# A gated mix of attention and SwiGLU on one core: q and k terms stored once and copied in DRAM, x split behind the last unit, one attention step a beat

## The chip, the cores and the metric

The kernel runs on one core of a Trainium2 chip. Its time is the device time of one execution, in microseconds (us). A core has five engines, each with its own instruction queue: TensorE (PE, matrix products; PEld is its weight load), VectorE (DVE), ScalarE (ACT), GpSimd (POOL) and SyncE (SP), which here issues every DMA. SBUF is the on-chip memory of 128 partitions, PSUM the eight banks that PE writes to; DRAM is the memory outside.

## The reference

```python
x = A_x                                              # 1 x 2048 x 576
g = sigmoid((x * gate_w).sum(-1, keepdims=True))
a = attention_with_memory(x, wq, wk, wv, wo, beta)   # 32 heads of 18, four segments of 512 rows
b = (silu(x @ w_gate) * (x @ w_up)) @ w_down         # 4608 hidden columns
return g * a + (1 - g) * b
```

In each segment a head computes a causal softmax attention over the segment's own 512 rows. It also reads a memory that was summed over the earlier segments, `phi(q) M / phi(q) z` with `phi(t) = t + 1` for positive t and `exp(t)` otherwise; `sigmoid(beta)` weighs the two.

## The kernel before

Single-precision products are made of parts: a number is split into a high part (rounded to PE's fast f32 format) and a rest, and three products, high x high, high x low, low x high, replace one. For the scores, q and k are split into three bf16 terms each, and six pairs of terms are stacked along the contraction: 6 x 18 = 108 rows for a head.

**Stage 1, projections** (lines 205 to 467). For each of four segments: nine chains (`qk`, line 248) of 14 matmuls of 512 columns make q and k for 128 columns of the weights; m = 4 holds 64 columns of q and 64 of k. `qk` makes the three bf16 terms `q3` of the chain (ACT, DVE, ACT, POOL; two buffers) and puts the writes of them to `stk` in DRAM on a list `late`. `stk` has six slots a row: for q the terms hi hi hi, mid mid, lo, and for k hi mid lo, hi mid, hi, so that slot by slot the six pairs meet. Each chain gives three writes (line 267), m = 4 six. `flush` (line 244) issues them from SP a chain later. Then eight value steps (`v_step`, line 272: 14 matmuls of 288 columns, half a head group and 128 rows each), between which stand the memory's products (`mem_step`, line 339). During the values the next segment's x is loaded and split, one chunk a step. In the last segment the eight x chunks of the feed-forward's first half are loaded instead (`x_first`, line 401) and split by 14 functions (`todo`).

**Stage 2, feed-forward and attention together** (lines 470 to 993). The rows are worked in two halves (segments 2 and 3, then 0 and 1). Each half has 36 units, one for each 128 hidden columns. A unit multiplies gate and up weights with x by a scheme of seven products (`seven`, line 883: six matmuls of 512 columns; `rest2` adds two) in place of eight; `w_make` (line 488) builds the seven weight operands in the first half and keeps them in DRAM, from which `w_fetch` takes them in the second. Sums of x chunks for the scheme are made by `x_sum` (POOL), their parts by `split` (ACT, DVE). Every third unit also starts 16 groups of the down projection (`down_group`, line 725: nine matmuls of 288 columns, then a DVE addition to `ya`).

The order is written out by hand. After each of a unit's eight products or pairs of them stands a `tick` (line 920), which calls `beat` (line 830). A beat first runs what was deferred to it (`due`: weight splits, loads, the splits of `hh` and `hl`), then up to SHARE[k] down groups, and between these it adds a credit of TICK[half][busy]; busy means that down groups are waiting. When the credit reaches 1, the next attention step is issued (`att_gen`, line 666). There are 339 steps; 320 of them have scores. When they are out, `c_open` (line 748) loads and splits the output weights over the next 13 beats. In beats 5 and 6, behind the Silu, a unit without groups takes no step (QUIET). With a SHARE of 3 the credit is added twice in a beat.

A step works on a fifth of a pair of heads. `t_bank` (line 606) makes up to 512 columns of transposed scores from blocks named in TPLAN, ACT takes their Exp into `pe` (line 616), POOL masks it, and DVE and POOL split it into two f16 parts (lines 689, 691). `s_bank` (line 565) makes scores for the row maxima of a later pair from blocks in SPLAN, which DVE reduces (line 579). Both share three PSUM banks in turn (5, 6, 7), so the scores of one step wait for the Exp of the step before. Every fifth step also issues 40 small matmuls with the values (lines 641, 643).

Between the halves `BREAK` = 10 beats without a unit run the last 16 groups, with a share of 2. During the first half's last unit and these beats `x_second` (line 849) loads, sums and splits x for the second half. Its `x_slot`s are those of the first half's x, which the last unit still reads.

**Stage 3** (lines 998 to 1028) adds the memory's part, projects with `wo` and mixes with the feed-forward.

In the built program SP uses eight DMA semaphores in turn: a DMA is not issued before the one eight places ahead of it has landed.

Of the kernel before, what the change touches and what calls it, by code (L numbers as in the profile page):

```python
# [20 lines left out]
P = 128  # L21
S = 2048
D = 576
# [18 lines left out]
HALF = ((2, 3), (0, 1))  # L42
TICK = ((0.2, 0.83), (0.64, 0.84))
QUIET = (5, 6)
# [11 lines left out]
def gated_mix(ctx, tc, xT, wf, wd, wv, wo, beta, cmask, ident, bmask, out):  # L56
# [146 lines left out]


    xs_of = {}
    with ExitStack() as st:
# [41 lines left out]
        def qk(s, m, u):  # L248
            t0 = s * L
            t = chain_tile()  # L250
            hi, lo = qw[m]
            products(t, w_stat(hi[:, u], lo[:, u]), x_side(*xs_of[s]))
            q3 = sp.tile([P, 3, L], BF, name="q3")
            qr = sp.tile([P, L], F32, name="qr", bufs=1)
            nc.scalar.activation(q3[:, 0], t, AF.Copy)
            nc.vector.tensor_sub(qr, t, q3[:, 0])  # L256
            nc.scalar.activation(q3[:, 1], qr, AF.Copy)  # L257
            nc.gpsimd.tensor_sub(q3[:, 2], qr, q3[:, 1])  # L258
            if m == 4 or (u == 0 and s > 0) or (u == 1 and s < 3):
                ph = sp.tile([P, L], F32, name=f"ph{m}{u}", bufs=2 if u or m == 4 else 1)  # L260
                phi[s, m, u] = ph
                nc.scalar.activation(ph, t, AF.Relu, scale=-1.0)
                nc.scalar.activation(ph, ph, AF.Exp, scale=-1.0)
                nc.vector.scalar_tensor_tensor(ph, t, 0.0, ph, op0=OP.max, op1=OP.add)
            parts = [(u, m * P, 0, P)] if m < 4 else [(0, 512, 0, 64), (1, 512, 64, 64)]
            for kind, r0, p0, n in parts:
                for c, m in ((0, 3), (3, 2), (5, 1)):
                    z = 3 - m
                    src = q3[p0:p0 + n, 0:m] if kind else q3[p0:p0 + n, z:z + 1].to_broadcast([n, m, L])
                    late.append((stk[kind, r0:r0 + n, c:c + m, t0:t0 + L], src))  # L270

# [150 lines left out]
        for s in range(NSEG):  # L422
            upd = upd_gen(s - 1) if s else None
            for n, (m, u) in enumerate(chains):
                if s == 0:
                    for z in loads.get(n, []):
                        z()
                    if n + 3 < 9:
                        q_split(*chains[n + 3])
                    if n in (6, 7):  # L430
                        v_split(n - 6)
                qk(s, m, u)
                flush(6 if m == 4 else 3)
                if upd is not None and n > 0:
                    next(upd, None)
                if s == 1 and n < 3:
                    masks(*((0, 3), (3, NT), (0, 0))[n])
# [8 lines left out]
            for n in range(8):  # L446
                hf, i = divmod(n, 4)
                flush()
                v_step(s, hf, i)
                if s:  # L450
                    mem_step(s, n // 2, n % 2)
                if s < 3:
                    if n == 0:
                        xs_of[s + 1] = x_tiles(s + 1)
                    if n < 5:
                        raws["x", n] = x_load(s + 1, n)
                    if 1 <= n < 6:
                        x_split(xs_of[s + 1], n - 1, raws["x", n - 1])
                else:
                    if n == 0:  # L460
                        wraw = {0: [w_load(0, u) for u in range(2)]}
                    if n == 4:
                        wraw[1] = [w_load(1, u) for u in range(2)]
                    for _ in range(2 if n in (1, 3, 5) else 1):
                        if len(todo) > 4:
                            todo.pop(0)()
        flush()


    with ExitStack() as st:  # L470
# [5 lines left out]
        def row_tile():  # L476
            return rw.tile([P, L], F32, name="row")


        wraw_of, wops, wrem = wraw, {}, {}  # L480

        def op_tile():
            return wop.tile([P, 2, 2, P], F32R, name="wo_")

        def rem_tile():
            return wop.tile([P, 2, P], F32R, name="wr_", bufs=3)

        def w_make(f):
            g, u = wraw_of.pop(f)
            ops, rem = [None] * 7, [None] * 2  # L490
            wops[0, f], wrem[0, f] = ops, rem
            a11, a12, a21, a22 = g[:, 0:2], g[:, 2:4], u[:, 0:2], u[:, 2:4]
            src = [a11, None, None, a12, None, None, a22]

            def total(j, p, q, sub=True):
                src[j] = rp.tile([P, 2, P], F32, name="ws", bufs=3)
                (nc.gpsimd.tensor_sub if sub else nc.gpsimd.tensor_add)(src[j], p(), q())

            def high(j):
                ops[j] = op_tile()  # L500
                nc.scalar.activation(ops[j][:, 0], src[j], AF.Copy)

            def low(j):
                nc.vector.tensor_sub(ops[j][:, 1], src[j], f32(ops[j][:, 0]))

            def rem_high(z, r):
                rem[z] = rem_tile()
                nc.scalar.activation(rem[z][:, 0], r, AF.Copy)

            def rem_low(z, r):  # L510
                nc.vector.tensor_sub(rem[z][:, 1], r, f32(rem[z][:, 0]))

            def keep(j):
                nc.sync.dma_start(wc[f, j], f32(ops[j]).rearrange("p a k n -> p (a k n)"))

            def rem_keep(z):
                nc.sync.dma_start(rc[f, z], f32(rem[z]).rearrange("p a n -> p (a n)"))

            todo = [(LEAD - 1, lambda: total(1, lambda: a21, lambda: a22, False)),
                    (LEAD, lambda: total(2, lambda: src[1], lambda: a11)),  # L520
                    (LEAD + 2, lambda: total(4, lambda: a11, lambda: a21)),
                    (LEAD + 3, lambda: total(5, lambda: a12, lambda: src[2]))]
            for j in range(7):
                todo += [(LEAD + j, lambda j=j: high(j)), (LEAD + j + 1, lambda j=j: low(j)),
                         (LEAD + j + 2, lambda j=j: keep(j))]
            for z, r in ((0, g[:, 4]), (1, u[:, 4])):
                o = LEAD + 4 + 2 * z
                todo += [(o, lambda z=z, r=r: rem_high(z, r)), (o + 1, lambda z=z, r=r: rem_low(z, r)),
                         (o + 2, lambda z=z: rem_keep(z))]
            return sorted(todo, key=lambda t: t[0])  # L530

# [14 lines left out]

        start = w_make(0)
        while start[0][0] < 8:
# [13 lines left out]
        stack_load(0)  # L562
        SPLAN = [[(0, 0, 3)], [(0, 1, 3)], [(0, 0, 2), (384, 0, 0)], [(0, 1, 2), (384, 1, 0)], [(0, 0, 1), (256, 1, 1)]]

# [38 lines left out]

        TPLAN = [[(0, 0)], [(1, 0)], [(0, 1), (0, 3)], [(1, 1), (1, 3)], [(0, 2), (1, 2)]]

# [48 lines left out]
        def o_step(g):  # L654
# [3 lines left out]
            nc.vector.reciprocal(rz, av[:, :, :, DH])  # L658
            nc.vector.tensor_mul(rz, rz, omg[:, 4 * b:4 * b + 4])
            ob = ap.tile([P, 4, 4 * DH], F32, name="ob", bufs=1)  # L660
# [169 lines left out]
        def beat(k=None, half=0):  # L830
# [4 lines left out]
            for n in range(max(share, 1)):  # L835
                if groups and n < share:
                    down_group(*groups.pop(0))
                if n % 2 or (k in QUIET and not busy):
                    continue
# [9 lines left out]
        def x_second(new, xs):  # L849
# [22 lines left out]
            todo = []  # L872
            for z, loads, at in ((0, ((1, 0), (3, 0), (0, 0), (2, 1)), 2), (1, ((0, 7), (1, 8), (3, 9), (2, 9)), 10)):
                todo += [(o, lambda z=z, q=q: load(z, q)) for q, o in loads]
                for o, j, what in ((0, 0, parts), (1, 1, total), (2, 1, parts), (3, 2, total), (3, 3, parts),
                                   (4, 2, parts), (4, 4, total), (5, 4, parts), (5, 6, total), (6, 5, parts),
                                   (6, 6, parts)):
                    todo.append((at + o, lambda z=z, j=j, what=what: what(z, j)))
            for b in range(2):
                todo += [(9, lambda b=b: rest_load(b)), (13 + b, lambda b=b: rest(b))]  # L880
            return sorted(todo, key=lambda t: t[0])
# [17 lines left out]
        for pos, (half, f) in enumerate(seq):  # L899
# [16 lines left out]
            for o, fn in plan:  # L916
                defer(o + 1, fn)
            step = [0]

            def tick():  # L920
# [38 lines left out]
            nc.scalar.activation(xx, a, AF.Copy)  # L959
            tick()  # L960
            seven(y, w[5], XO[5], False, False)
            rest2(y, wr[0], XS[1])
            nc.scalar.activation(sg1, y, AF.Silu)  # L963
            nc.scalar.activation(sg0, sg0, AF.Silu)
            tick()
# [12 lines left out]
            if f == FT - 1:  # L978
                groups += feed(half, f)
                if half == 0:  # L980
                    for _ in range(BREAK):
                        beat()
                    XO, XS = X2, XS2
# [92 lines left out]
```

## Time and profile before

| | |
|---|---|
| median of 3 runs | 1948.53 us (1942.0 to 1951.9) |
| the profiled execution | 1951.22 us; its span is 1949.5 us |
| mean granted TensorE clock | 0.984 |
| projections, 0 to 259 us | PE is busy in 226.4 of 259 us |
| half one with its break | 259 to 1076 us |
| half two | 1076 to 1860 us |
| the end | 1860 to 1950 us |
| DMA | 344.96 MB in 227878 packets, mean 177 GB/s |

The span runs from the first to the last instruction. A line of a group reads: line, engine, operation, what it writes and reads, count, busy time, mean of one, idle time of the engine before it with what ended most of that. A line of waits reads: who waited for whom, us in total, how often, the longest. A line of the order of time reads: start, length, engine, line, operation, out<-in, count, and in brackets the idle time before it with what ended it. "PE busy" is a model of pipelined matmuls; a PE that is busy is not always at its peak.

### The profile page before, as it was taken

To read this page: it belongs to the slowest core of one execution; us is meant where nothing else is said; L and a number is where in the kernel's file an instruction comes from. 1 tells how busy PE (TensorE), PEld (TensorE's weight loads), DVE (VectorE), ACT (ScalarE), POOL (GpSimd) and SP (SyncE) were. 2 spreads that over 40 slices of the span, in tenths; PEclk is the share of its full clock that TensorE was granted. 3 is DMA by queue.
4 is the path that set the end of the run, shared out by engine and by line. 5 is a ranking of instruction groups with operands and counts; after the bars stand their busy time and mean duration, and the time that the engine had idled before them with its cause. 6 is when DMAs were issued, how large, how long until landed. Compare 5 with 4: busy or idle time off the path is not lost.

```text
span 1949.5 us, 35977 instructions
## 1 busy us (share of the span) xinstructions
PE 1845.1 (95%) x12508; PEld 1554.6 (80%) x12508; DVE 1274.4 (65%) x3064; ACT 947.2 (49%) x1786; POOL 856.5 (44%) x1214
## 2 busy tenths in 40 slices
PE   7899889999999999999997999999999999999999
PEld 6788778778877877888786787787787788778899
DVE  5355377787787778788877766666666766443355
ACT  5555463665466466556654544435444544432211
POOL 2323352454545555555555655555555555400021
PEclk9999999999999999999998999999999999999999
DMA  7565666664565456356645645545544643564444
GB/s 246 180 203 182 214 249 205 216 220 134 180 232 178 154 199 222 134 191 236 216 145 189 208 140 148 156 141 146 152 143 145 184 131 107 167 198 154 137 156 140
DMA packets 227878, 344.96 MB, mean 177 GB/s; under 512 B 38576, under 2 KB 123696, under 8 KB 227696
## 3 DMA queue, kind: packets, MB, share of 16 engines
q1 hardware_dynamic: 227696, 342.66, 54.2%
q8 instruction: 99, 1.62, 0.4%
q14 instruction: 83, 0.68, 0.1%
HBM read 194.33 MB, written 148.24 MB: 176 GB/s over the span
## 4 chain that ended last, share of the span: by engine, by line
PE 73%; DVE 7%; ACT 7%; DMA 5%; issue 4%; POOL 2%; SPq 1%; ACTq 0%; DVEq 0%; POOLq 0%
PE bank L887 28%; PE bank L735 23%; PE bank L893 6%; PE bank L127 5%; PE bank L572 3%; PE bank L612 3%; PE bank L641 2%; ACT L616 1%; DMA xo<-in_xT_dram 1%; PE bank L643 1%; ACT pe L616 1%; DVE xo L105 1%; PE bank L304 1%; POOL p L691 1%; DVE qr L256 1%
## 5 line engine op out<-in xcount | busy, mean ns | idle before, releaser
L691 POOL TENSOR_TENSOR p<-pe,p 128x512 f16<-128x512 f32 x320 | 372.4, 1164 | 598.3 <-DVE p L689 542.4
L735 PE MATMUL bank<-dw,hh 128*128 128x288 f32 x2304 | 482.3, 302 | 21.5 <-DVE ya L740 10.4
L735 PEld LDWEIGHTS bank<-dw,hh 128*128 128x128 f32 x2304 | 378.9, 190 | 45.8 <-DVE ya L740 15.8
L616 ACT ACTIVATE pe<-bank 128x512 f32<-128x512 f32 x320 | 190.4, 596 | 338.2 <-PE bank L612 287.9
L735 PE MATMUL bank<-dw,hl 128*128 128x288 f32 x1152 | 342.1, 297 | 1.1 <-DVE hl L105 1.1
L740 DVE TENSOR_TENSOR ya<-bank,ya 128x288 f32<-128x288 f32 x352 | 160.1, 456 | 228.2 <-PE bank L735 225.2
L579 DVE CUSTOM_DVE_ANT_0 scr<-bank,cm 128x512 bf16<-128x512 f32 (+3 forms) x512 | 248.7, 486 | 10.1 <-PE bank L572 3.3
L735 PEld LDWEIGHTS bank<-dw,hl 128*128 128x128 f32 x1152 | 218.7, 190 | 1.7 <-DVE hl L105 1.7
L689 DVE CAST p<-pe 128x512 f16<-128x512 f32 x320 | 166.4, 521 | 2.8 <-POOL pe L624 2.8
L572 PE MATMUL bank<-kst,qst 108*128 108x512 bf16 (+3 forms) x512 | 126.8, 301 | 30.2 <-ACT pe L616 28.5
L612 PE MATMUL bank<-qst,kst 111*128 111x512 bf16 (+3 forms) x512 | 151.3, 306 | 0.0
L624 POOL TENSOR_SCALAR_AFFINE_SELECT pe<-pe 128x256 f32<-128x256 f32 (+1 forms) x320 | 136.6, 427 | 15.2 <-ACT pe L616 13.3
L955 ACT ACTIVATE row<-bank 128x512 f32<-128x512 f32 x72 | 43.0, 597 | 140.3 <-PE bank L893 140.2
L105 DVE TENSOR_TENSOR hl<-row,hh 128x512 fp32r<-128x512 f32 x72 | 52.5, 729 | 82.9 <-ACT hh L104 82.9
L612 PEld LDWEIGHTS <-kst 111*128 111x128 bf16 x512 | 49.4, 98 | 71.0 <-issue 53.3
L968 DVE TENSOR_TENSOR bank<-bank,row 128x512 f32<-128x512 f32 x72 | 50.3, 698 | 80.8 <-ACT row L963 80.2
L127 PE MATMUL bank<-xo,qhi 128*128 128x512 f32 x288 | 93.6, 406 | 7.4 <-ACT xo L104 5.1
L792 POOL TENSOR_TENSOR o<-o,me 128x576 f32<-128x576 f32 x12 | 17.1, 1428 | 189.0 <-DMA me<-med 180.8
L616 ACT ACT_TABLE_LOAD x59 | 75.7, 1283 | 44.7 <-PE bank L612 42.4
L944 ACT ACTIVATE bank<-bank 128x512 f32<-128x512 f32 x72 | 42.0, 583 | 98.4 <-PE bank L887 87.8
L258 POOL TENSOR_TENSOR q<-qr,q 128x512 bf16<-128x512 f32 x36 | 41.9, 1164 | 106.9 <-ACT q L257 106.0
L959 ACT ACTIVATE bank<-bank 128x512 f32<-128x512 f32 x72 | 41.9, 582 | 96.5 <-PE bank L887 96.5
(2083 smaller groups left out, 4354.4 us busy)
## 6 DMA issues: line engine op xcount, KB each, us to landing
raw<-in_wf_dram SPq DMA_DIRECT2D x72, 320.0 KB
dc<-dw SPq DMA_DIRECT2D x36, 576.0 KB
dw<-dc SPq DMA_DIRECT2D x36, 576.0 KB
qst<-stk SPq DMA_DIRECT2D x64, 216.0 KB
kst<-stk SPq DMA_DIRECT2D x64, 216.0 KB
stk<-q SPq DMA_DIRECT2D x32, 384.0 KB
draw<-in_wd_dram SPq DMA_DIRECT2D x36, 288.0 KB
stk<-q SPq DMA_DIRECT2D x32, 256.0 KB
```

The lines of the kernel that those rows point to most:

```text
L127: nc.tensor.matmul(t, st[n], mv[n], start=(n == 0), stop=(n == 13))
L572: nc.tensor.matmul(t[:, c:c + w], qs[:KR, pr, P * i:P * i + P], ks[:KR, pr, 0:w], start=True, stop=True)
L579: nc.vector.tensor_tensor_reduce(scr[:, :w], t[:, c:c + w], cm[:, L - w:L], 1.0, -3.0e38, OP.add, OP.max, m[:, k:k + 1])
L612: nc.tensor.matmul(t[:, c:c + w], ks[:KR + 3, pr, P * j:P * j + P], qs[:KR + 3, pr, P * j:L], start=True, stop=True)
L616: nc.scalar.activation(pe, t, AF.Exp, scale=SCALE)
L624: nc.gpsimd.affine_select(d, d, pattern=pat, compare_op=OP.is_ge, fill=0.0, base=0, channel_multiplier=-1)
L689: nc.vector.tensor_copy(p1, pe)
L691: nc.gpsimd.tensor_sub(p2, pe, p1)
L735: nc.tensor.matmul(t, p, q[:, cs], start=(n == 0), stop=(n == 3 * CH - 1))
L740: nc.vector.tensor_add(ya[:, i, cs], t, ya[:, i, cs])
L887: nc.tensor.matmul(t, w[:, p, z], x[z][:, q], start=first and n == 0, stop=last and n == 5, skip_group_check=True)
L893: nc.tensor.matmul(t, w[:, p], xs, start=False, stop=p == 1, skip_group_check=True)
```

## The change

1. `q3` of a k chain is stored in the opposite order (lo mid hi). Each chain now writes its three terms to slots 0 to 2 in one DMA; m = 4 writes q in one and k in three. New `copies(s)` fills slots 3 and 4, and 5, of q and k by four DMAs from DRAM to DRAM. They are issued behind value steps 4 to 7 for segments 0 to 2, and in units 2 to 5 of the feed-forward for segment 3. The six pairs of terms are the same.
2. In the last segment's values no x split is done behind step 0 and two behind each of steps 1 to 5. `w_make(0)`, the first unit's weights, moves from behind the values into steps 3 to 7 (its functions moved up in the file unchanged).
3. `beat`: without waiting groups, credit is added once a beat. TICK is changed with it.
4. SPLAN and TPLAN: in three banks the 128-column block comes before the 384-column block.
5. `x_second`: loads and splits are later, the splits all behind the first half's last unit; the first beat of the break takes no down group.
6. Silu of `sg0` is issued a product earlier, ahead of that of `sg1`.
7. The small product for `rz` goes from DVE to POOL.

The order of the program's instructions on PE differs only by item 4 and by where steps and groups fall; the number of matmuls is the same. SP issues 56 DMAs fewer (72 writes less, 16 copies more).

```diff
-TICK = ((0.2, 0.83), (0.64, 0.84))
+TICK = ((0.25, 0.83), (0.6, 0.8))
...
-            nc.scalar.activation(q3[:, 0], t, AF.Copy)
-            nc.vector.tensor_sub(qr, t, q3[:, 0])
+            z0, z2 = (2, 0) if u else (0, 2)
+            nc.scalar.activation(q3[:, z0], t, AF.Copy)
+            nc.vector.tensor_sub(qr, t, q3[:, z0])
             nc.scalar.activation(q3[:, 1], qr, AF.Copy)
-            nc.gpsimd.tensor_sub(q3[:, 2], qr, q3[:, 1])
+            nc.gpsimd.tensor_sub(q3[:, z2], qr, q3[:, 1])
...
-            parts = [(u, m * P, 0, P)] if m < 4 else [(0, 512, 0, 64), (1, 512, 64, 64)]
-            for kind, r0, p0, n in parts:
-                for c, m in ((0, 3), (3, 2), (5, 1)):
-                    z = 3 - m
-                    src = q3[p0:p0 + n, 0:m] if kind else q3[p0:p0 + n, z:z + 1].to_broadcast([n, m, L])
-                    late.append((stk[kind, r0:r0 + n, c:c + m, t0:t0 + L], src))
+            if m < 4:
+                late.append((stk[u, m * P:m * P + P, 0:3, t0:t0 + L], q3))
+            else:
+                late.append((stk[0, 512:D, 0:3, t0:t0 + L], q3[0:64]))
+                for z in range(3):
+                    late.append((stk[1, 512:D, 2 - z, t0:t0 + L], q3[64:128, z]))
+
+        def copies(s):
+            t0 = s * L
+            r = []
+            for kind in range(2):
+                for c, m in ((3, 2), (5, 1)):
+                    z = 3 - m if kind else 0
+                    r.append((stk[kind, :, c:c + m, t0:t0 + L], stk[kind, :, z:z + m, t0:t0 + L]))
+            return r
...
-                flush(6 if m == 4 else 3)
+                flush(4 if m == 4 else 1)
...
-                    for _ in range(2 if n in (1, 3, 5) else 1):
+                    for _ in range(2 if n else 0):
                         if len(todo) > 4:
                             todo.pop(0)()
+                    if n == 3:
+                        start = w_make(0)
+                    for _ in range((0, 0, 0, 0, 3, 3, 6, 6)[n]):
+                        if start[0][0] < 8:
+                            start.pop(0)[1]()
+                if n > 3 and s < 3:
+                    nc.sync.dma_start(*copies(s)[n - 4])
...
-        SPLAN = [[(0, 0, 3)], [(0, 1, 3)], [(0, 0, 2), (384, 0, 0)], [(0, 1, 2), (384, 1, 0)], [(0, 0, 1), (256, 1, 1)]]
+        SPLAN = [[(0, 0, 3)], [(0, 1, 3)], [(384, 0, 0), (0, 0, 2)], [(384, 1, 0), (0, 1, 2)], [(0, 0, 1), (256, 1, 1)]]
...
-        TPLAN = [[(0, 0)], [(1, 0)], [(0, 1), (0, 3)], [(1, 1), (1, 3)], [(0, 2), (1, 2)]]
+        TPLAN = [[(0, 0)], [(1, 0)], [(0, 1), (0, 3)], [(1, 3), (1, 1)], [(0, 2), (1, 2)]]
...
-            nc.vector.tensor_mul(rz, rz, omg[:, 4 * b:4 * b + 4])
+            nc.gpsimd.tensor_mul(rz, rz, omg[:, 4 * b:4 * b + 4])
...
-                if n % 2 or (k in QUIET and not busy):
+                if n % 2 or (not busy and (n or k in QUIET)):
                     continue
...
-            for z, loads, at in ((0, ((1, 0), (3, 0), (0, 0), (2, 1)), 2), (1, ((0, 7), (1, 8), (3, 9), (2, 9)), 10)):
+            for z, loads, at in ((0, ((0, 3), (1, 3), (3, 4), (2, 5)), 8), (1, ((0, 11), (1, 12), (3, 12), (2, 13)), 13)):
                 todo += [(o, lambda z=z, q=q: load(z, q)) for q, o in loads]
-                for o, j, what in ((0, 0, parts), (1, 1, total), (2, 1, parts), (3, 2, total), (3, 3, parts),
-                                   (4, 2, parts), (4, 4, total), (5, 4, parts), (5, 6, total), (6, 5, parts),
-                                   (6, 6, parts)):
+                for o, j, what in ((0, 0, parts), (0, 1, total), (1, 1, parts), (1, 2, total), (1, 3, parts),
+                                   (2, 2, parts), (2, 4, total), (2, 6, total), (3, 4, parts), (3, 5, parts),
+                                   (4, 6, parts)):
                     todo.append((at + o, lambda z=z, j=j, what=what: what(z, j)))
             for b in range(2):
-                todo += [(9, lambda b=b: rest_load(b)), (13 + b, lambda b=b: rest(b))]
+                todo += [(9, lambda b=b: rest_load(b)), (16 + b, lambda b=b: rest(b))]
...
+            if half == 0 and 2 <= f < 6:
+                defer(4, lambda f=f: nc.sync.dma_start(*copies(NSEG - 1)[f - 2]))
...
+            nc.scalar.activation(sg0, sg0, AF.Silu)
             seven(y, w[5], XO[5], False, False)
             rest2(y, wr[0], XS[1])
             nc.scalar.activation(sg1, y, AF.Silu)
-            nc.scalar.activation(sg0, sg0, AF.Silu)
...
-                    for _ in range(BREAK):
-                        beat()
+                    for n in range(BREAK):
+                        beat(None if n else 0)
```

More of the change, by code (lines that the diff above doesn't have):

```diff
@@ L202, in d_load, with op_tile, rem_tile, w_make @@
         return r
+    wraw_of, wops, wrem = {}, {}, {}
+    def op_tile():
+        return wop.tile([P, 2, 2, P], F32R, name="wo_")
+    def rem_tile():
+        return wop.tile([P, 2, P], F32R, name="wr_", bufs=3)
+    def w_make(f):
+        g, u = wraw_of.pop(f)
+        ops, rem = [None] * 7, [None] * 2
+        wops[0, f], wrem[0, f] = ops, rem
+        a11, a12, a21, a22 = g[:, 0:2], g[:, 2:4], u[:, 0:2], u[:, 2:4]
+        src = [a11, None, None, a12, None, None, a22]
+        def total(j, p, q, sub=True):
+            src[j] = rp.tile([P, 2, P], F32, name="ws", bufs=3)
+            (nc.gpsimd.tensor_sub if sub else nc.gpsimd.tensor_add)(src[j], p(), q())
+        def high(j):
+            ops[j] = op_tile()
+            nc.scalar.activation(ops[j][:, 0], src[j], AF.Copy)
+        def low(j):
+            nc.vector.tensor_sub(ops[j][:, 1], src[j], f32(ops[j][:, 0]))
+        def rem_high(z, r):
+            rem[z] = rem_tile()
+            nc.scalar.activation(rem[z][:, 0], r, AF.Copy)
+        def rem_low(z, r):
+            nc.vector.tensor_sub(rem[z][:, 1], r, f32(rem[z][:, 0]))
+        def keep(j):
+            nc.sync.dma_start(wc[f, j], f32(ops[j]).rearrange("p a k n -> p (a k n)"))
+        def rem_keep(z):
+            nc.sync.dma_start(rc[f, z], f32(rem[z]).rearrange("p a n -> p (a n)"))
+        todo = [(LEAD - 1, lambda: total(1, lambda: a21, lambda: a22, False)),
+                (LEAD, lambda: total(2, lambda: src[1], lambda: a11)),
+                (LEAD + 2, lambda: total(4, lambda: a11, lambda: a21)),
+                (LEAD + 3, lambda: total(5, lambda: a12, lambda: src[2]))]
+        for j in range(7):
+            todo += [(LEAD + j, lambda j=j: high(j)), (LEAD + j + 1, lambda j=j: low(j)),
+                     (LEAD + j + 2, lambda j=j: keep(j))]
+        for z, r in ((0, g[:, 4]), (1, u[:, 4])):
+            o = LEAD + 4 + 2 * z
+            todo += [(o, lambda z=z, r=r: rem_high(z, r)), (o + 1, lambda z=z, r=r: rem_low(z, r)),
+                     (o + 2, lambda z=z: rem_keep(z))]
+        return sorted(todo, key=lambda t: t[0])
     xs_of = {}
@@ L460, in gated_mix @@
                     if n == 0:
-                        wraw = {0: [w_load(0, u) for u in range(2)]}
+                        wraw_of[0] = [w_load(0, u) for u in range(2)]
                     if n == 4:
-                        wraw[1] = [w_load(1, u) for u in range(2)]
-                    for _ in range(2 if n in (1, 3, 5) else 1):
+                        wraw_of[1] = [w_load(1, u) for u in range(2)]
+                    for _ in range(2 if n else 0):
                         if len(todo) > 4:
                             todo.pop(0)()
+                    if n == 3:
[5 more added lines that the diff above has]
+                    nc.sync.dma_start(*copies(s)[n - 4])
         flush()
@@ L477, in row_tile @@
             return rw.tile([P, L], F32, name="row")
[L480 to L530, printed above, removed]
         def w_fetch(f):
@@ L545, in w_fetch @@
             return [(j + 2 + late * (j == 6), lambda j=j: one(j)) for j in range(7)] + [(8, lambda: two(0)), (9, lambda: two(1))]
-        start = w_make(0)
         while start[0][0] < 8:
```

## The prediction

> **What bounds the kernel now.** I read the busy times first, then the stages by windows, then the waits of PE stage by stage, then the order of time where PE waits. The first line says that PE is busy for 95% of the span; no other engine passes 65%. So an edit pays only where it removes PE time or a wait of PE, and 1949.5 - 1845.1 = 104.4 us of waits exist at all, in the records.
>
> ```profile
> PE 1845.1 (95%) x12508; PEld 1554.6 (80%) x12508; DVE 1274.4 (65%) x3064; ACT 947.2 (49%) x1786; POOL 856.5 (44%) x1214
> ```
>
> The windows cut this by stage (us, then busy time of PE, PEld, DVE, ACT, POOL, the granted clock, DMA share, GB/s):
>
> ```profile
> 0.00:64.00 64.00, 49.84 (x241) 42.37 (x242) 30.97 (x48) 38.03 (x70) 16.57 (x25) 0.95 0.72 233
> 225.00:259.00 34.00, 23.81 (x161) 23.05 (x159) 22.60 (x54) 17.40 (x41) 19.87 (x19) 0.90 0.60 201
> 259.00:275.00 16.00, 14.21 (x52) 11.03 (x53) 10.44 (x25) 10.34 (x22) 10.15 (x15) 0.79 0.78 276
> 302.00:1022.00 720.00, 692.59 (x4707) 577.25 (x4707) 552.20 (x1333) 405.26 (x805) 360.90 (x518) 0.99 0.56 189
> 1022.00:1076.00 54.00, 41.69 (x300) 35.66 (x299) 39.23 (x86) 23.12 (x41) 31.93 (x37) 0.84 0.56 189
> 1076.00:1692.00 616.00, 594.17 (x4496) 481.98 (x4495) 410.56 (x1063) 292.08 (x479) 337.37 (x508) 1.00 0.51 152
> ```
>
> The reader is to see where PE is not full: the first segment (14 us idle), the last values and the first unit (12 us idle, clock 0.90 and 0.79), the break between the halves (12 us, clock 0.84), and about 4% of either half. The waits of PE name the causes:
>
> ```profile
> PE bank L572 <- ACT pe L616: 28.5, 26, 2.2
> ...
> PE bank L735 <- ACT hh L104: 7.7, 2, 7.5
> ```
>
> **The sum**, against the profiled execution's own 1951.2 us (span 1949.5); the median of the three runs, 1948.5, lies 2.7 lower.
>
> *Terms once, copied later (segments 0 to 2).* SP issues 12 writes a segment in place of 30. In segment 0 nine writes hold SP from 45.95 to 52.03, x loads behind them; ACT waits 2.9 us for x, and PE 5.6 + 0.9 us for a bank that ACT had to empty. Later segments show the same queue (11 writes in 11.0 and 12.3 us) with about 1 us of PE waits each. The m=4 rows still wait for POOL (49.1), so x goes out only about 1 us sooner by SP alone; more comes from the bytes ahead of it, now half. Against that, the copies: 3.54 MB a segment (1152 rows x 3 x 1 KB), issued from the fifth value step. No copy from DRAM to DRAM is in the trace. The nearest rows move 284 GB/s at a DMA share of 0.85 (0 to 34 us), 334 at full share: 10.6 us a segment if bytes count once, 21 if reading and writing count apart. Left for them are four value steps, 12 us. So in the slow case they outlast the values by 9 us, and the mask loads (POOL already waits 1.8 and 1.5 us for them) and the first term writes stand behind. I take a gain of 2 us; bounds 7 gained and 12 lost.
>
> *Last values and first unit.* Before:
>
> ```profile
> 227.25 5.58 SPq L246 DMA_DIRECT2D stk<-q  x9
> ...
> 236.79 0.63 ACT L104 ACTIVATE xo<-xr 128x512 fp32r<-128x512 f32 x1 [5.43 <-DMA xr<-in_xT_dram]
> ...
> 240.22 1.61 PE L350 MATMUL bank<-Mm,ph 128*128 128x114 f32 x6 [4.67 <-DVE om L357]
> ```
>
> Nine writes go ahead of eight x loads (issued from 232.93); ACT stands at the first split, DVE behind it, PE behind DVE. Now five writes are ahead, the first split comes a value step later, and the first unit's weights are made during the values, not after them (PE waits 3.9 + 1.8 us for them at 258.9 and 261.8). Almost without waits eight steps take 23.5 us (segment 2, 164.5 to 188.0), and a unit takes 11.3 (1784.0 to 1795.3): 34.8 against 50.1 (224.8 to 274.9), so 15.3 can be had. ACT, DVE and POOL each get about 20 us of work in 24 us of values, and the weights arrive behind 2 MB of x, so I take 8 (4 to 13).
>
> *A step a beat.* I worked the credits through. Half one gets 153 steps (155 before), the second half the rest; attention ends in unit 33 of half two, not 27. In half two, six idle units (4, 5, 13, 14, 22, 23) took two steps in the last beat. Each looks like this:
>
> ```profile
> 1391.11 1.28 ACT L616 ACT_TABLE_LOAD   x1 [1.60 <-PE bank L612]
> 1392.40 0.60 ACT L616 ACTIVATE pe<-bank 128x512 f32<-128x512 f32 x1
> ...
> 1393.05 0.38 PE L572 MATMUL bank<-kst,qst 108*128 108x512 bf16 x1 [1.91 <-ACT pe L616]
> ```
>
> The second step's scores need the bank that the first step's Exp empties, and that Exp first loads its table. The six cost 10.7 us of the 15.7 that PE waits there for `pe` (1076 to 1692). Now an idle unit has one step a beat at most, so they go; next to be late is a step in the last beat followed by one in the first (0.3 to 0.6 us each; by the credits 13 times, 20 before). I take 11 of the window's 21.8 idle us (3 to 17). In half one such waits (8 times, 12.9 us, 2.2 at most) stand where a unit with groups has steps in beats 0 and 1, or in 0 after 7. By the credits that happens 5 times now, 8 before: 12.9 x 3/8 = 5, and 1 more for the lower clock after each: 6 (1 to 10). The last four copies go here, one a unit behind other transfers; a full-rate 3.5 us each does not reach the next unit's weights.
>
> *Order of the blocks (SPLAN, TPLAN).* A block of 128 columns no longer ends a step; three of five steps change, 192 of 320. The same 1024 columns and six products after them, twice in the trace:
>
> ```profile
> 1313.84 0.32 PE L612 MATMUL bank<-qst,kst 111*128 111x384 bf16 x1
> 1314.00 0.27 PE L572 MATMUL bank<-kst,qst 108*128 108x256 bf16 x1
> 1314.11 0.22 PE L612 MATMUL bank<-qst,kst 111*128 111x128 bf16 x1
> 1314.17 0.27 PE L572 MATMUL bank<-kst,qst 108*128 108x256 bf16 x1
> 1314.20 1.61 PE L887 MATMUL bank<-xo,wo__16557 128*128 128x512 f32 x6
> 1315.64 0.62 PE L893 MATMUL bank<-xs,wr__16686 128*128 128x512 f32 x2
> ```
>
> From the first block to what follows the six products is 1.80 us with 128 inside, and 1.90 with 128 last (1396.25 to 1398.15, same view). Over 30 and 109 such places the medians are 1.82 and 1.89. My reading: a load of f32 weights (190 ns at line 735) is not hidden behind so short a block, a bf16 load (98 ns at line 612) nearly is: 0.06 us from the 128 to the next. 192 x 0.07 = 13.4 us; where PE waits anyway it is lost, so 10 (0 to 13).
>
> The Trainium skill ("TensorE: Matmul & The Clock Gate", Back-to-back issue gap) gives about 81 ns for each 128-column matmul in a stream of load and matmul pairs, wherever it stands. By that rule the place is worth nothing. The 0.06 us above disagrees, so I keep the 10.
>
> *Break.* PE waits 7.5 us for `hh` (1038.66) because ACT stood at x splits that wait for POOL and DMA; later 2.9 us for DVE. A unit (11.3), 16 groups (19.2: a unit with them took 30.5, 1753.5 to 1784.0) and 7.5 steps at 0.86 (a unit with five took 15.6, 1106.8 to 1122.4) make 37, against 53.9 from one `p5` to the next (1021.8 to 1075.7). Moved behind the unit, the splits put about 27 us of DVE work (14 x 0.69, 16 x 0.46, steps) beside 26 of PE, so DVE is late next. I take 6 (0 to 13).
>
> *The rest.* Silu ahead: no table load more or fewer, 0.6 us of ACT off a path that PE rarely sees; `rz` on POOL: 32 tiny operations. 0 (2 either way). Output weights are now loaded and split in the last two units: the 4 us that PE idles at 1692 to 1754 move there, 0 (5 lost if they run past the end).
>
> 2 + 8 + 11 + 6 + 10 + 6 = 43: 1908 by the profiled execution, **1906** by the median.
>
> **Rivals.** (a) The beat does not pay: each Exp still loads its table, so the waits per step stay and only spread. Both step terms gone: 1923. For it: single steps wait too, 0.3 to 0.6 us. (b) The short block costs the same anywhere: 1916. (c) All terms near their better ends, as each wait removed also lifts the clock: 1884. (d) Nothing lasts: one engine's wait takes over from another's, within 0.5%. For it: POOL waits 542 us for DVE `p`, so all are chained; against it, DVE is busy only 65%. (e) Slower: copies crawl. An SP wait on a landing is known (26.9 us, at most 4.1, for `mxd`), but here 1 MB lies behind it. Copies have the 12 us and some 25 idle us of the next segment's transfers; beyond 37 us (under 96 GB/s, a third of the rate above) two buffers of `q3` fill, and ACT and PE stop. Three segments of 60 us lose 3 x 23 = 69 there: 1975. It decides against the change from 51 us a segment.
>
> The Trainium skill ("DMA: Bandwidth & Descriptors", Why a DMA increments its semaphore by 16 and not by 1) has a transfer use as many engines, up to 16, as divide its slowest dimension; 576 rows would get all 16, which speaks against (e). No run here shows it yet.
>
> **Chances.** Forecast (1890 to 1915) 0.47; (a) 0.17; (b) 0.10; (c) 0.12; (d) 0.07; (e) 0.07. Under 0.5% (9.7 us) a measurement cannot tell a change from none. Faster by more: 0.86, within 0.07, slower 0.07. The range leaves out (d), (e) and half of (c): 1882 to 1936.
>
> **To be seen afterwards.** Term copies landing within 15 us of issue; no 4.7 us wait at the memory products and no wait for the first unit's weights; the break under 48 us; no two Exps of a beat in idle units, and `pe` waits under 15 us in all; 1.82 in place of 1.89 behind a step; the last steps near 1790, where POOL falls idle. I am wrong if PE's busy time stays at 1845 while its idle time stays at 104, or if ACT waits for `q3` buffers behind the copies.

## The result and the profile after

The changed kernel takes 1935.5 us (median of 6 runs, 1931.4 to 1939.2) against 1949.4 for the one before on the same chip: a ratio of 0.9934, 95% interval 0.9913 to 0.9955. That is 13 us less where 43 were forecast. The profiled execution took 1935.9 us (span 1933.9; before 1951.2 and 1949.5). Executions of one kernel differ in how long the clock was low: 23 of the kernel before, in one set of runs, go from 1939.3 to 1951.2 us at mean granted clocks of 0.990 to 0.984, and the profile of before (0.984) stands at the long end, so a difference of two profiles is not yet a difference of two kernels.

PE's line of the busy times, the stages by windows (the stages shown of before, at the changed kernel's own times; the last ends about where the unit stands that stood at 1692 before) and the longest waits of PE, after the change:

```profile
PE 1836.5 (95%) x12508; PEld 1553.5 (80%) x12508; DVE 1233.2 (64%) x3032; ACT 964.8 (50%) x1800; POOL 861.5 (45%) x1246
```

```profile
0.00:60.50 60.50, 48.67 (x241) 41.48 (x242) 31.00 (x48) 37.74 (x70) 16.60 (x25) 0.97 0.57 186
231.40:265.40 34.00, 25.79 (x168) 24.27 (x166) 22.98 (x53) 17.63 (x41) 22.46 (x21) 0.89 0.55 185
265.40:281.40 16.00, 13.24 (x45) 9.56 (x44) 10.74 (x27) 10.29 (x24) 8.57 (x13) 0.81 0.72 250
308.60:1022.00 713.40, 684.71 (x4655) 572.29 (x4653) 534.02 (x1306) 402.20 (x799) 360.55 (x526) 1.00 0.58 195
1022.00:1074.60 52.60, 43.91 (x308) 37.40 (x305) 40.39 (x85) 24.95 (x45) 32.71 (x36) 0.87 0.58 197
1074.60:1650.00 575.40, 566.27 (x4152) 469.02 (x4151) 352.49 (x942) 273.59 (x441) 278.14 (x436) 1.00 0.53 161
```

```profile
PE bank L751 <- DVE ya L756: 13.7, 10, 2.5
PE bank L367 <- ACT kt L376: 12.3, 5, 2.9
PE bank L588 <- ACT pe L632: 11.0, 14, 2.1
PE bank L413 <- DVE om L420: 6.8, 4, 4.9
```

PE is busy 8.6 us less and idle 97.4 us, 7.0 less. The first segment is 3.5 us shorter, the stretch of half two idles 9 us where it idled 22, and `pe` costs 11.0 us in place of 28.5. But `kt` rises from 3.8 to 12.3, the memory products still wait 4.9 us once, and the break still holds nearly 9 idle us. From the first `p5` of each unit the difference (after less before) is: stage 1 to the first unit +5.4 us, units 0 to 2 +1.0, unit 3 +5.6, units 4 to 34 of half one -11.8, the break -1.3, half two -18.6, the end +4.1; in all -15.7.

Where stage 1 loses is in the chain that ended last (the longest pieces of 60 to 330 us; start, us, what), and in ACT's order of time: its third `q` copy of segments 1, 2 and 3, and the weight split of unit 3.

```profile
70.50 7.65 DMA stk<-q
...
198.43 6.39 DMA stk<-q
306.70 8.58 DMA wc<-wo__2881
```

```profile
78.25 0.60 ACT L309 ACTIVATE q<-bank 128x512 bf16<-128x512 f32 x1 [4.31 <-DMA stk<-q]
...
141.38 0.60 ACT L309 ACTIVATE q<-bank 128x512 bf16<-128x512 f32 x1 [3.16 <-DMA stk<-q]
...
204.93 0.60 ACT L309 ACTIVATE q<-bank 128x512 bf16<-128x512 f32 x1 [4.20 <-DMA stk<-q]
...
315.36 0.42 ACT L226 ACTIVATE wo__2992<-raw 128x256 fp32r<-128x256 f32 x1 [6.12 <-DMA wc<-wo__2881]
```

The reader is to see a buffer that is free only when a write has landed, 6 to 9 us after its issue. That the write stands behind the copies is argued here; the run that moves the copies tests it. Before, the same four places waited 0.44, 0, 1.96 and 1.60 us.

### The profile page after: what moved, and what is told of

The parts are those of the page before. It is cut to its first block, busy times and chain, and to the rows that moved or that the text cites. A ratio compares the mean times of both kernels' runs of the same rounds, so it can differ in the third digit from the quotient of the medians.

```text
span 1933.9 us, 35781 instructions
## 1 busy us (share of the span) xinstructions
PE 1836.5 (95%) x12508; PEld 1553.5 (80%) x12508; DVE 1233.2 (64%) x3032; ACT 964.8 (50%) x1800; POOL 861.5 (45%) x1246
## 4 chain that ended last, share of the span: by engine, by line
PE 67%; DVE 10%; ACT 8%; DMA 7%; issue 5%; POOL 2%; SPq 1%; DVEq 0%; ACTq 0%; POOLq 0%
PE bank L903 24%; PE bank L751 22%; PE bank L127 5%; PE bank L909 4%; PE bank L628 3%; PE bank L588 3%; PE bank L657 2%; DMA xo<-in_xT_dram 1%; PE bank L659 1%; ACT L632 1%; ACT L979 1%; DVE xo L105 1%; PE bank L367 1%; DVE qr L310 1%; DMA stk<-q 1%
## 5 line engine op out<-in xcount | busy, mean ns | idle before, releaser
L705 DVE CAST p<-pe 128x512 f16<-128x512 f32 x320 | 155.2, 485 | 0.0
L977 ACT ACTIVATE bank<-bank 128x512 f32<-128x512 f32 x72 | 41.9, 582 | 95.7 <-PE bank L903 90.3
L659 PE MATMUL bank<-v,p 128*128 128x38 bf16 x1280 | 77.1, 181 | 5.4 <-POOL p L707 5.2
```

The source lines that it names most:

```text
L705: nc.vector.tensor_copy(p1, pe)
```

## The experiments

Theory after the result: steps and block order gain about what was forecast, and the copies give a part of it back in stage 1 and unit 3. Rivals: the copies are hidden and the lag comes from other edits; the parts take each other's waits. First four parts were built alone on the kernel before, then the copies were moved and the other parts built alone; the combinations came last. Microseconds are ratios times 1946, the median of before in these runs; every ratio is against the kernel before, with its 95% interval.

**terms**: the three-row writes, `copies` and both places that issue them, alone.

```diff
-                for c, m in ((0, 3), (3, 2), (5, 1)):
-                    z = 3 - m
-                    src = q3[p0:p0 + n, 0:m] if kind else q3[p0:p0 + n, z:z + 1].to_broadcast([n, m, L])
-                    late.append((stk[kind, r0:r0 + n, c:c + m, t0:t0 + L], src))
+            if m < 4:
+                late.append((stk[u, m * P:m * P + P, 0:3, t0:t0 + L], q3))
...
+                if n > 3 and s < 3:
+                    nc.sync.dma_start(*copies(s)[n - 4])
+            if half == 0 and 2 <= f < 6:
+                defer(4, lambda f=f: nc.sync.dma_start(*copies(NSEG - 1)[f - 2]))
```

> The kernel before with the terms part alone: three term rows written a segment, the other three copied in DRAM during the values (segment 3's in four units of half one), flush counts to match. Theory now: the copies start late in the values and, with x, value and memory transfers, fill the transfer queue some 9 us beyond them, so the first term writes of the next segment land late and ACT waits for a free q buffer in the third chain: about 4 us in each of segments 1 to 3 (0.4, 0 and 2.0 before), and the weight stores of a unit stand behind a copy in half one (ACT 6 us in unit 3, 1.6 before). Segment 0 gains 3.5 us. So the first unit starts 4 to 7 us later than before, unit 3 takes 3 to 6 us more, and the time is 5 to 12 us longer than before. The forecast said 2 us shorter (12 longer to 7 shorter for segments 0 to 2, nothing for segment 3's copies). A rival: the copies are hidden and the lag of the changed kernel comes from the other edits: then 3 to 4 us shorter.

Measured: 1.0066 [1.0045, 1.0086], 12.8 us longer (8.8 to 16.7). ACT waits 4.03 us (77.40) and 3.89 us (205.15) for `stk<-q`, in segment 2 not at all, and 4.75 us for the weight store in unit 3; PE's waits for `kt`, behind ACT, are 11.5 us. The mechanism of the theory holds, with one of its three buffer waits missing, and the hidden copies fall; the loss is just above the 5 to 12 us that it gave. By the profiles the first unit starts 4.0 us later than before, as expected, and unit 3 takes 2.3 us more, under the 3 to 6 expected. That profile is the shortest of five executions (1954.6 to 1963.2), so it does not show where all of the 12.8 us lie. Part is the clock: over all executions its mean is 0.9846 against 0.9865, some 8 us more at half clock, worth about 4 (an estimate from these means).

**values**: the first unit's `w_make` within the values and the later x split, alone (the diff's edits of that loop).

> The kernel before with the part on the last values alone: first unit's weights made within the values, the first x split a value step later. Theory now: nothing much to be had, as the x transfers still land after PE needs them and the extra splits and sums slow DVE and POOL: the first unit starts within 3 us of before (either way). The forecast said 8 us earlier (4 to 13). A rival: the part is worth its 8 us and is hidden in the changed kernel by the late queue.

Measured: 1.0002 [0.9989, 1.0015]. PE's waits from 222 to 276 us, kernel values:

```profile
PE bank L403 <- DVE om L410: 4.6, 1, 4.6
PE bank L892 <- ACT bank L949: 3.5, 1, 3.5
PE bank L892 <- DVE wo__2430 L229: 1.8, 1, 1.8
```

Before they were 4.7, 3.9 and 1.8. The first is as long as before and stands one value step later, since ACT still waits for x (2.89 us at 236.13). The wait for the first weights is gone, and in its place PE waits for ACT's copy of a bank, which stands behind four x splits (2.17 us) that now come after the weights. In the 44.35 us that end with the first unit's `p5`, PE idles 11.3 us in place of 12.0: the waits moved. That `p5` stands 4.7 us earlier than in the profile of before, more than the 3 expected, but 3.2 of these are there when the values begin, ahead of the edit; from there to the `p5` it takes 40.1 us in place of 41.6.

**beat**: the step rule and the credits, alone.

```diff
-TICK = ((0.2, 0.83), (0.64, 0.84))
+TICK = ((0.25, 0.83), (0.6, 0.8))
-                if n % 2 or (k in QUIET and not busy):
+                if n % 2 or (not busy and (n or k in QUIET)):
```

> The kernel before with the step rule alone: at most one step a beat in idle units, and the changed credits. Forecast: 11 us less in half two and 6 less in half one, 17 in all, PE's waits for pe under 15 us (28.5 before). Theory now: 10 to 14 less in half two, about 5 less in half one, and 2 to 5 lost behind the last unit, since attention ends six units later and the output weights come late: 12 to 16 us less. Rival (a): the waits only spread: no change.

Measured: 0.9867 [0.9846, 0.9888], 26 us less, more than either theory gave; rival (a) falls. Half two, first for before (1076 to 1692), then for beat over about the same units, and beat's waits for `pe`:

```profile
1076.00:1692.00 616.00, 594.17 (x4496) 481.98 (x4495) 410.56 (x1063) 292.08 (x479) 337.37 (x508) 1.00 0.51 152
```

```profile
1060.00:1641.00 581.00, 574.18 (x4214) 472.35 (x4213) 371.00 (x969) 277.69 (x447) 277.59 (x427) 1.00 0.53 162
```

```profile
PE bank L572 <- ACT pe L616: 8.5, 10, 2.1
```

The stretch is short partly because steps moved behind it (units 27 to 34 take 21 us longer), so the idle time is read: 21.8 becomes 6.8. Over the whole of half two idle time falls by 16.4 us and `pe` by 20.0 in the kernel. In half one idle time falls by 4.3 us. The rest is the clock: over all executions of these runs its mean rises from 0.9865 to 0.9898, which is 53 us at half clock before and 39 here, so 6 to 7 us of time (an estimate from these means). The two profiles show more, 62 and 35 us, since they lie at opposite ends of their kernels' executions. One of the places that went, in the kernel before, in windows of 3.4 us (PE busy first, the granted clock third from the end):

```profile
361.40:364.85 3.45, 1.38 (x7) 0.88 (x7) 2.85 (x6) 3.42 (x8) 1.74 (x3) 1.00 1.03 396
364.85:368.26 3.41, 3.41 (x13) 2.97 (x12) 2.83 (x8) 1.16 (x3) 3.18 (x7) 0.51 1.01 345
368.26:371.67 3.41, 3.41 (x21) 2.88 (x21) 3.18 (x9) 0.60 (x1) 1.87 (x3) 0.99 0.99 358
```

A wait of 2.07 us for `pe` lies in the first; in the second PE is never idle, at half clock. The same product in the second and in the third, in PE's order of time:

```profile
367.34 0.44 PE L735 MATMUL bank<-dw,hl 128*128 128x288 f32 x1
...
369.10 0.29 PE L735 MATMUL bank<-dw,hl 128*128 128x288 f32 x1
```

**order**: SPLAN and TPLAN alone.

> The kernel before with the new order of blocks alone (SPLAN, TPLAN). Forecast and theory now: 0.07 us a step in 192 of 320 steps, so 13 us of PE's busy time, 10 to 13 us of the time. Rival (b): the short block costs the same in any place: no change. A third: PE's busy time falls but the waits of PE grow by as much, since the pe and the maxima come in another order: under 5 us.

Measured: 0.9976 [0.9963, 0.9989], 4.7 us less. The saving at a step is there: from the first block to what follows the six products 1826 and 1837 ns (medians of 76 and 33 places) against 1894 and 1896. PE's busy time falls by 7.7 us, of the 13 forecast, and its idle time rises by 2.3; the waits for `pe` are 31.5 us in place of 28.5. So rival (b) falls, and the third theory is half right.

**spread**: the changed kernel, its copies of segments 0 to 2 behind the third to sixth chain of the next segment, segment 3's in twelve pieces from unit 4 on.

```diff
-                if n > 3 and s < 3:
-                    nc.sync.dma_start(*copies(s)[n - 4])
+                if s and 3 <= n < 7:
+                    nc.sync.dma_start(*copies(s - 1)[n - 3])
-            if half == 0 and 2 <= f < 6:
-                defer(4, lambda f=f: nc.sync.dma_start(*copies(NSEG - 1)[f - 2]))
+            if half == 0 and 4 <= f < 16:
+                defer(4, lambda f=f: nc.sync.dma_start(*pieces[f - 4]))
```

> The changed kernel with its copies elsewhere: those of segments 0 to 2 behind the third to sixth chain of the next segment, where the transfer queue is nearly empty, and segment 3's in twelve pieces, one a unit from unit 4 of half one. Theory: with the queue free behind the values, ACT's waits of 3 to 4 us for a q buffer in the third chains go, and so do the 6 us that unit 3 of half one waits for a weight store: 10 to 16 us less than the changed kernel, 23 to 30 less than before. A rival: copies cost wherever they stand, since their 14 MB go through the same queue: within 4 us of the changed kernel.

Measured: 0.9856 [0.9837, 0.9874], 28 us less than before. Same bytes, same queue, other hours (and segment 3's copies in smaller pieces): 15 us better than the changed kernel. ACT's waits from 0 to 260 us, its third `q` copy of segment 1, then unit 3's weight split:

```profile
ACT q L309 <- DMA stk<-q: 1.2, 2, 0.9
```

```profile
73.56 0.59 ACT L309 ACTIVATE q<-bank 128x512 bf16<-128x512 f32 x1
```

```profile
300.14 0.42 ACT L226 ACTIVATE wo__2991<-raw 128x256 fp32r<-128x256 f32 x1 [1.37 <-DMA wc<-wo__2881]
```

12.0 us of `stk<-q` have become 1.2 (6.4 before), and 6.12 us of the store 1.37; PE's waits for `kt` go from 12.3 to 3.4. In segment 1 SP issues the first chain's write at 70.22, and at 70.50 in the changed kernel, so it was not SP that was late: with no copies ahead the third `q` copy starts at 73.56 without a wait, with them it starts at 78.25. Of the 16.5 us between the two profiles 11.3 lie before the first unit and 5.3 in unit 3. That settles the place as the cause in stage 1. In unit 3 the copies are gone and the wait with them; what their later place and what their smaller pieces would do each was not tried.

**break**: `x_second` and the break's first beat alone.

> The kernel before with the part on the break alone: x of the second half split behind the last unit, no groups in the break's first beat. Forecast: 6 us less (13 to 0), with DVE late next. Theory now, from the changed kernel's break (1.3 us shorter than before, 1.5 us longer than with the step rule alone): no gain, within 3 us of before. A rival: it is worth its 6 us here, and the step rule had already taken them in the changed kernel.

Measured: 0.9985 [0.9972, 0.9998], 2.9 us less; within the 3 us of the later theory, half of the forecast's 6. PE's waits in its break:

```profile
PE bank L735 <- DVE ya L740: 3.9, 4, 1.7
PE bank L735 <- ACT hh L104: 3.3, 1, 3.3
```

7.5 us for `hh` became 3.3, while `ya` went from 3.3 to 3.9, and two more waits of 0.7 and 0.8 us for `p` and `ya` came up: DVE is late next.

**silu**: Silu of sg0 ahead and `rz` on POOL; **ahead** and **rzpool** are the two by themselves.

> The kernel before with two edits alone: the Silu of sg0 issued a product ahead, and rz multiplied on POOL. Forecast: no change (2 either way). Theory now: the four other parts give about 13 less copies, 27 for steps and 4 for order, 18 in all, the changed kernel 13; what is left, 5 us, is lost by the break or by these two, and if by these it shows here as 3 to 6 us more. A rival: parts that each save waits of PE overlap, and these two cost nothing: within 2 us of before.

> The kernel before with the Silu of sg0 issued a product ahead, nothing else. The two small edits together lost 4.7 us. Theory: it is this one, 3 to 6 us more: the Silu and its table load now stand between an Exp of the attention and the copies that free PE's banks. A rival: it is rz on POOL, and this one is within 2 us of before.

> The kernel before with rz multiplied on POOL in place of DVE, nothing else. Theory: within 2 us of before (32 small operations). A rival: 3 to 6 us more, as POOL gets to it late and ob with it behind POOL's queue.

Measured: silu 1.0024 [1.0012, 1.0035], ahead 1.0015 [1.0004, 1.0027], rzpool 0.9992 [0.9980, 1.0004]. The Silu alone costs 2.9 us (0.8 to 5.3), `rz` nothing that can be told. In the profile of silu PE waits 3.5 us for DVE's sum behind that Silu, in that of ahead 1.7 and in that of before 0.3. How the rest arises is open.

**pair** (step rule and order), **three** (with the break as well), **best** (three with the terms part, its copies placed as in spread).

> The kernel before with the step rule and the order of blocks, nothing else. If the two add: 27 + 4 = 31 us less than before, 1915. A rival: the shorter steps are lost to waits once the step rule is in: 27 less, 1919. By the forecast's terms 27 less as well (17 + 10), but from other shares.

> The kernel before with step rule, order of blocks and break, nothing else. Measured so far: 32 us less for the first two together, 2.9 for the break alone. If parts add: 35 us less, 1910. A rival: the break's part was won only from waits that the step rule has taken away: 32 less, 1913.

> The kernel before with step rule, order, break, and the terms part with its copies behind the third to sixth chain of the next segment (segment 3's in twelve pieces in half one). Theory: the terms part loses only by where its copies stood; placed so it gives 2 to 5 us of segment 0 and of the fewer writes: 37 to 40 us less than before, 1905 to 1908. A rival, from the changed kernel with its copies moved (28 less, against a sum of the other parts alone of 28): well placed the terms part is worth nothing: within 2 us of the kernel without it (three).

Measured: pair 0.9830 [0.9812, 0.9848], three 0.9832 [0.9817, 0.9846], best 0.9806 [0.9789, 0.9823]. Step rule and order add (33 us). Beside them the break is worth nothing: its `hh` wait falls from 5.2 to 2.5 us and its `hl` wait from 2.7 to 0.5, and `ya` rises from 2.0 to 6.2 in the same stretch. Well placed copies bring 5 us more (1914.9 to 1910.1; 38 us less than before by the ratio), as the theory had it and more than the rival's 2; the intervals overlap, so this gain is likely and not shown. best beats both kernels: 1910.1 us, 25 less than the changed one.

## Why the prediction was wrong

The parts alone add to the result: terms +12.8, values +0.4, steps -25.9, order -4.7, break -2.9, Silu and `rz` +4.7: -15.6, against -12.8 measured, with some 8 us of doubt on the sum by the six intervals. So no large loss is hidden between the parts; the terms of the sum were wrong. From the 43 forecast to these 16, terms take away 15, the values 8, the order 5, the break 3, Silu and `rz` 5, and the steps give 9 back.

- *Terms once, copied later* is the step that failed. It took 2 us gained and got 13 lost, at the edge of its own bound of 12 for segments 0 to 2. Not the rate: while the copies of segment 1 ran, with other transfers among them, the queue was full and moved 349 GB/s, against the 334 that the working took.

```profile
122.00:140.00 18.00, 15.13 (x80) 13.01 (x79) 8.44 (x25) 8.12 (x18) 4.49 (x5) 0.95 1.03 349
```

The copies go out from 120.57 on. PE's last value product ends at 124.5; the store of these values (issued at 130.71) and the next segment's first term write (134.78) stand behind the copies, and the queue empties at 140. The working named this as its slow case and still took a gain. It also gave the next segment "some 25 idle us" before two `q3` buffers fill. But the third chain needs the first chain's write landed: ACT was ready for its `q` copy at 138.2, 8.3 us after that of the first chain (129.88), and started it at 141.38. The limit was there, not at 37 us. The Trainium skill ("DMA: Bandwidth & Descriptors", Queues, rings and completion order) has each engine consume a queue's descriptors in ring order; the trace agrees, with a 384 KB write landing 7.65 us after its issue at 70.50, where with no copies ahead the third `q` copy ran 3.34 us after the issue.
- "Does not reach the next unit's weights" failed as well: not the weight loads stood behind segment 3's copies but the stores of the weights before (8.58 us at 306.70), which must land before ACT may write into a ring of six. It cost unit 3 5.6 us.
- *Last values* (8 taken, 0 measured, 2.5 either way): only the weights' wait was moved; x arrives no sooner for the step that needs it, and ACT has the same splits to do a little later.
- *A step a beat* (17 taken, 26 measured): the waits were the right ones; idle time fell by 16.4 and 4.3 us in the halves against 11 and 5 taken. The clock, put at 1 us, gave 6 to 7.
- *Order* (10 taken, 5 alone, 7 beside the steps): the mechanism and its size are right where six products follow, 0.06 to 0.07 us, but PE's busy time fell by 7.7 us and not by 13, and waits took part of that; where the rest went is not shown. The Trainium skill's 81 ns ("TensorE: Matmul & The Clock Gate", Back-to-back issue gap) are for a stream of load and matmul pairs of 128 columns. The prediction read from them that the place would be worth nothing, and rightly kept its own measurement: here, among blocks and products of other kinds, 1894 ns became 1826.
- *Break* (6 taken): DVE late next, as said; 3 alone, 0 beside the steps. *The rest* (0 taken): 3 us lost to the Silu, and the end 1.8 us longer with the step rule alone.

Of the signs named, `pe` under 15 us, 1.82 behind a step and the last steps near 1790 (POOL's last `p` ends at 1786.7) came true. The 4.7 us at the memory products stayed (4.9), PE still waits 1.8 us for the first unit's weights, and the break takes 52.6 us, not under 48. The ACT waits for `q3` behind the copies, which were to prove the forecast wrong, came.

## What to carry to other kernels

A transfer that nobody waits for is not free: ask what is issued behind it on its queue, and which buffers come free only when that has landed. The count of buffers, not the queue's idle time, says how long the delay may be. A wait of PE that lasts two microseconds is to be priced with the clock that follows it, and each part of a change is best tried alone, since here three parts that gain stood beside two that lose.

## What the runs showed that was not expected

The clock record switches PE to half speed in pieces of 3.41 us. In all fourteen profiles, from 300 to 1850 us, each such drop (one to three pieces long) follows a stretch of 3.41 us in which PE stood idle for 1.57 us or more, and no such stretch with more than 1.9 idle us was without one. Between these two figures some had a drop behind them and some had none. So a wait of some 2 us costs up to 1.7 us again. The Trainium skill ("TensorE: Matmul & The Clock Gate", Why this matters for your kernels) warns of gaps over about 3 us; here about half of 3.41 us was enough.

The copies from DRAM to DRAM ran in packets of 1 KB with a median of 46 ns each. The 349 GB/s count each byte once, so reading and writing did not add up as in the slow case of the working.
